# Attention and a gated expert on one core: the first span's later output products in hi and lo parts, two weight splits a block sooner, and a last output that ends row group by row group

## The chip, the core and the metric

The kernel runs on one core of a Trainium2 chip. A core has a matrix engine (TensorE, PE in the profile, with its weight loads as PEld), VectorE (DVE), ScalarE (ACT) and GpSimd (POOL), a queue engine for transfers (SyncE, SP), and 16 DMA engines between device memory and the on-chip memory. TensorE writes its sums into PSUM banks, from which the other engines read them. Each engine works through its own list of instructions in order and waits where an input isn't there yet. The metric is the device time of one execution in microseconds (us); lower is better.

## The reference

Linear attention over q, k and v, then a gated feed-forward layer over its output:

```python
def _attn_ref(q, k, v):                       # (8, 8, 576, 64) each
    q_s = np.exp(q - np.max(q, axis=-1, keepdims=True))
    q_s = q_s / (np.sum(q_s, axis=-1, keepdims=True) + 1e-09)
    k_s = np.exp(k - np.max(k, axis=2, keepdims=True))
    k_s = k_s / (np.sum(k_s, axis=2, keepdims=True) + 1e-09)
    kv = np.einsum('bhsd,bhse->bhde', k_s, v)
    return np.einsum('bhsd,bhde->bhse', q_s, kv).astype(np.float32)

def _moe_ref(x, w_gate, w_val, w_out):        # x: 4608 tokens x 512; d_ff 1536
    gate = 1.0 / (1.0 + np.exp(-(x @ w_gate)))
    val = x @ w_val
    return (gate * val @ w_out).astype(np.float32)
```

The attention's output of (8, 8, 576, 64) is laid out as 4608 tokens of 512 features. The weights arrive as float64 words.

## The kernel before

**Tiling.** The tokens are worked in 9 spans of 512 (`NW = 9`, `T = 512`), each of 4 row groups of 128 (`NT = 4`). The 1536 hidden features are 12 blocks of 128 (`NJ = 12`), or 6 pairs (`NS = 6`).

**First span and later spans differ.** The first span (w = 0) works while the weights arrive. It runs over the 12 blocks j = 0 to 11. `g1_0(j)` makes the gate and the value product of a block from plain float32 weights (line 650; 8 products, which the profile shows as 16 records), `g_sig_0(j)` (658, ScalarE) and `g_mul_0(j)` (662, VectorE) form the block's hidden values `h_0[j]`, and `g2_0(j)` (677) multiplies them with the block of the output weights, in float32, into four accumulators, one for each row group. The loop issues `g2_0(j - 1)` after `g1_0(j)`.

The later spans (w = 1 to 8) run over the pairs in `g1` (695) and `g2` (763). There every number is held as two parts that TensorE takes at its faster type float32r: hi, the number rounded by a cast on ScalarE, and lo, the remainder from a subtraction on VectorE. A product of two numbers is then three products, hi by hi, hi by lo and lo by hi. `g1` also uses a scheme of seven half-size products on sums of weight quarters (`w_sums`) instead of eight.

**What the first span does besides.** During the 12 blocks the weights are narrowed from float64 and got ready for the later spans, in this order around the change:

- `w_low`, `w_top`, `w_join` (lines 146, 153, 168, 175) narrow a block of the gate and value weights; `wo_low`, `wo_top`, `wo_join` a block of the output weights. Of these `w_top` and `wo_top` are on ScalarE, the others on VectorE.
- `wo_hi(j)` (224, ScalarE) and `wo_lo(j)` (228, VectorE) make the hi and lo parts of a block of output weights in a buffer `wo_hl` (two of them), `wo_store` writes them to device memory from POOL's queue; `wo_save` is `wo_lo` and `wo_store`.
- For each of the 6 pairs p, `w_sums(p)` (260, VectorE) makes four sums of weight quarters, and a split makes hi and lo parts of the four sums and of the three quarters used as they are: `split_hi(p)` (284, ScalarE) and `split_lo(p)` (289, VectorE), six casts and six subtractions. The parts of the sums go through one buffer, `s_sb`, and are stored from POOL's queue. The dictionary `splits` says in which block each split stands; `w_sums` of a split stands at the end of the block before.
- `beside_first(j)` and `after_first(j)` prepare span 1: `qT_split` (540, a cast on ScalarE; 541, a subtraction on VectorE), `x_mm` (565) and its eviction `x_ev` (573), transposes `qf_tr` (527), the k part of batch 2 (`k_max` 330, `k_sum` 337).
- The last two blocks, 10 and 11, are written out after the loop, with the sums and the split of the last pair (`w_sums(5)`, `split_hi(5, ...)`, `split_lo(5, ...)`; its six parts are `FIRST`, four `SUMS` and `LAST`) and the seven activations' parts `c_subs` (609), `c_split_hi` (625), `c_split_lo` (629) that span 1 begins with.

**What sets the order.** The order is written out by hand: each call appends its instructions to the engines' lists, and an engine never takes a later instruction first. Buffers come from pools with a fixed number of them; three PSUM banks (`ps_gv`) serve the gate and value products, the transposes and later `g1`'s three accumulators, and a new use waits until an earlier one has been read.

**The end.** `acc_out(w)` (669, 670) copies the four accumulators of a span on ScalarE and issues one transfer each from SP. In `g2` the loop over the two blocks of a pair is outside that over the four row groups, so that in the last pair the four accumulators are all finished by the last 12 products.

Of the kernel before, what the change touches and what calls it, by code (L numbers as in the profile page):

```python
# [52 lines left out]
def attn_moe(ctx: ExitStack, tc: tile.TileContext, qf, qn, qT, k, kT, v, wg, wv, wo, out):  # L53
# [156 lines left out]
    def wo_top(j):  # L210
        if j % 2 == 0:
            wo_t[j // 2] = wtpool.tile([P, 2, DM], F32, name="wo_t")
        if not wo_on_vector(j):
            narrow_sign(wo_raw[j])
        narrow_abs(wo_raw[j], wo_t[j // 2][:, j % 2])

    def wo_join(j):
        narrow_join(wo_raw.pop(j), wo_t[j // 2][:, j % 2])
# [3 lines left out]
    def wo_hi(j):  # L222
        wo_out[j] = t = whpool.tile([P, 2, DM], F32R, name="wo_hl")
        nc.scalar.copy(out=t[:, 0], in_=wo_t[j // 2][:, j % 2])

    def wo_lo(j):
        t = wo_out[j]
        nc.vector.tensor_tensor(
            out=t[:, 1], in0=wo_t[j // 2][:, j % 2], in1=t[:, 0].bitcast(F32), op=ALU.subtract
        )  # L230

    def wo_store(j):
        t = wo_out[j]
        nc.gpsimd.dma_start(out=wo_dram[j], in_=t.rearrange("p h e -> p (h e)").bitcast(F32))
# [43 lines left out]
    def split_hi(p, parts=(*SUMS, FIRST, LAST)):  # L278

        if p not in a_w:  # L280
            a_w[p] = apool.tile([P, 3, 2, 2, 2 * P], F32R, name="a_w", tag=f"a{p}")
        for part in parts:
            o, x = split_of(p)[part]
            nc.scalar.copy(out=o[:, :, 0], in_=x)

    def split_lo(p, parts=(*SUMS, FIRST, LAST)):
        for part in parts:
            o, x = split_of(p)[part]
            nc.vector.tensor_tensor(
                out=o[:, :, 1], in0=x, in1=o[:, :, 0].bitcast(F32), op=ALU.subtract  # L290
            )
            if part in SUMS:
                i = part - 1
                nc.gpsimd.dma_start(
                    out=s_dram[p][:, i * 8 * P:(i + 1) * 8 * P],
                    in_=s_sb[:, i].rearrange("p h n e -> p (h n e)").bitcast(F32),
                )
# [307 lines left out]
    def c_subs():  # L605

        def sub(i, x, y):
            c_32[i] = t = ring.tile([P, 2, HT], F32, name="ring")
            nc.vector.tensor_tensor(out=t, in0=x, in1=y, op=ALU.subtract)

        sub(T1, quarter(0, 1), quarter(0, 0))
        sub(T2, quarter(1, 1), c_32[T1])
        sub(T3, quarter(1, 1), quarter(0, 1))
        sub(T4, quarter(1, 0), c_32[T2])
# [29 lines left out]
    def g1_0(j):  # L644
# [8 lines left out]
                )  # L653
        gate[j] = ps

    def g_sig_0(j):
        h_0[j] = two.tile([P, T], F32, name="h_0", tag="h_lo")
        nc.scalar.activation(h_0[j], gate[j][0], AF.Sigmoid)

    def g_mul_0(j):  # L660
        g = h_0[j]
        nc.vector.tensor_tensor(out=g, in0=gate.pop(j)[1], in1=g, op=ALU.mult)

    def acc_new(w):
        acc[w] = [ps_acc.tile([P, DM], F32, name="acc") for _ in range(NT)]

    def acc_out(w):
        for m in range(NT):
            nc.scalar.copy(out=x_32[:, m], in_=acc[w][m])
            nc.sync.dma_start(out=out[w * T + m * P:w * T + (m + 1) * P], in_=x_32[:, m])  # L670
        del acc[w]

    def g2_0(j):
        if j == 0:
            acc_new(0)
        for m in range(NT):
            nc.tensor.matmul(  # L677
                acc[0][m], lhsT=h_0[j][:, m * P:(m + 1) * P], rhs=wo_t[j // 2][:, j % 2],
                start=(j == 0), stop=(j == NJ - 1),
            )  # L680
        if j == NJ - 1:
            acc_out(0)

# [70 lines left out]
    def g2(w, at):  # L754
        p = step(w, at)
        if at == 0:
            acc_new(w)
        h, o = h_hl.pop((w, p)), wo_hl.pop((w, p))
        for i in range(2):
            for m in range(NT):  # L760
                sl = slice(m * P, (m + 1) * P)
                for lh, rh in ((0, 0), (0, 1), (1, 0)):
                    nc.tensor.matmul(  # L763
                        acc[w][m], lhsT=h[lh][:, i, sl], rhs=o[i][:, rh],
                        start=(at == 0 and i == 0 and lh == 0 and rh == 0),
                        stop=(at == NS - 1 and i == 1 and lh == 1),
                    )
        if at == NS - 1:
            acc_out(w)

# [257 lines left out]
    for t in range(5):  # L1028
        k_load(1, t)

    splits = {2: 0, 5: 1, 7: 2, 9: 3, 10: 4, 11: 5}
    for j in range(NJ - 2):
        g1_0(j)
        beside_first(j)
        split = splits.get(j)
        if split is not None:
            split_hi(split)
        if j == 0:
            g_sig_0(j)
        else:  # L1040
            wo_hi(j - 1)
            g_mul_0(j - 1)
        w_top(j + 2)
        if j > 0:
            g_sig_0(j)
        w_join(j + 1)
        wo_top(j + 1)
        wo_join(j)
        if j + 3 < NJ:
            w_low(j + 3)  # L1050
        wo_low(j + 2)
        if j > 0:
            wo_save(j - 1)
        if j + 3 < NJ:
            load_wo(j + 3)
        if j + 5 < NJ - 1:
            load_w(j + 5)
        if j == 7:
            load_w(NJ - 1)
        if split is not None:  # L1060
            split_lo(split)
        if j + 1 in splits:
            w_sums(splits[j + 1])
# [8 lines left out]
    beside_first(j)  # L1072
    wo_hi(j - 1)
    g_mul_0(j - 1)
    wo_top(j + 1)
    split_hi(4)
    wo_lo(j - 1)
    wo_store(j - 1)
    w_join(j + 1)
    wo_join(j)  # L1080
    g_sig_0(j)
    split_lo(4)
    k_max_read(2)
    c_split_hi(B11)
    wo_hi(j)
    g_mul_0(j)
    wo_join(j + 1)
    g2_0(j - 1)

    g1_0(j + 1)  # L1090
    w_sums(5)
    split_hi(5, (FIRST,))
    g_sig_0(j + 1)
    split_hi(5, SUMS)
    c_subs()
    load_next(1, 5, range(2))
    c_split_lo(B11)
    split_lo(5, (FIRST,))
    split_lo(5, SUMS[0:1])
    c_split(T1)  # L1100
    g_mul_0(j + 1)
    split_lo(5, SUMS[1:2])
    c_split(T2)
    c_split(B21)
    wo_save(j)
    split_lo(5, SUMS[2:3])
    c_split(T3)
    split_lo(5, SUMS[3:4])
# [1 line left out]
    split_hi(5, (LAST,))  # L1110
    split_lo(5, (LAST,))
    c_split(T4)
    wo_hi(j + 1)
    wo_lo(j + 1)
    g2_0(j)
    for t in range(2, 5):
        v_load(2, t)

    def wo_next(w, at):
# [71 lines left out]
```

## Time and profile before

| | |
|---|---|
| median of 3 runs | 944.86 us (944.68 to 947.01) |
| profiled execution, its own time | 946.96 us |
| its span, first to last instruction | 945.2 us |
| mean granted TensorE clock | 0.994 |
| TensorE busy (PE) | 933.5 us, 99% of the span |
| VectorE busy | 626.4 us, 66% |
| ScalarE busy | 485.4 us, 51% |
| GpSimd busy | 176.5 us, 19% |
| first span's last output product of the loop, block 9, starts | at 148.91 us |
| span 1's products start | at 162.64 us |

The busy shares are means over the whole span. In the first span, some 160 us, VectorE and ScalarE are much busier than in the rest. The chain of waits that the page gives is followed back from the last instruction; a line of it says how much of the span lies on an engine's work. Line numbers of rows are those of the kernel before.

### The profile page before, as it was taken

Reading aid. Unit: us, or ns where it says so; the run is one execution under the profiler, and the core shown is the slowest. Engines: PE = TensorE matmul, PEld = TensorE weight load, DVE = VectorE, ACT = ScalarE, POOL = GpSimd, SP = SyncE. Lnnn points to the kernel's source line nnn. Section 1 sums busy time; section 2 is a strip of 40 time slices with the busy share of each in tenths; the row PEclk is TensorE's granted clock in tenths of the full one; section 3 lists DMA queues with packets and bytes.
Section 4 is the critical chain, followed back from the end, with each engine's and each line's share of the span. In section 5 each row is a group of like instructions: output and inputs, shape, how many; then the busy total and the mean of one; then the engine's idle time right before and its main releaser. Section 6 shows DMA issues by size and latency. Waiting matters only on the chain.

```text
span 945.2 us, 15707 instructions
## 1 busy us (share of the span) xinstructions
PE 933.5 (99%) x6062; PEld 808.2 (86%) x6062; DVE 626.4 (66%) x1017; ACT 485.4 (51%) x822; POOL 176.5 (19%) x330
## 2 busy tenths in 40 slices
PE   6999999999999999999999999999999999999998
PEld 5545545899999999999999999999999999999997
DVE  8899879874767477755776568556856664654242
ACT  4799786635455445544563456254725443543222
POOL 0011112222121212212221122112212122222220
PEclk8999999999999999999999999999999999999999
DMA  9996576999699969996999699978997789858661
GB/s 323 328 392 226 210 288 237 362 342 272 185 372 320 264 183 354 335 266 208 333 331 283 204 309 344 287 246 252 351 266 229 221 258 314 238 177 262 212 212 67
DMA packets 94249, 256.74 MB, mean 272 GB/s; under 512 B 13600, under 2 KB 15904, under 8 KB 94176
## 3 DMA queue, kind: packets, MB, share of 16 engines
q0 software_dynamic: 46016, 167.27, 56.6%
q1 hardware_dynamic: 48160, 88.48, 30.9%
q8 instruction: 48, 0.79, 0.4%
q14 instruction: 25, 0.20, 0.1%
HBM read 227.15 MB, written 28.56 MB: 271 GB/s over the span
## 4 chain that ended last, share of the span: by engine, by line
PE 98%; DVE 1%; DMA 1%; ACT 0%; issue 0%; SPq 0%; DVEq 0%
PE gv L695 49%; PE acc L763 28%; PE gv L650 9%; PE acc L677 4%; PE at L405 3%; PE gv L565 2%; PE at L565 1%; PE acc L392 1%; DMA lent<-k_in 1%; PE acc L589 0%; PE gv L527 0%; DVE lent L480 0%; DVE q_m L473 0%; DVE lent L963 0%; ACT lent L384 0%; ACT lent L484 0%
## 5 line engine op out<-in xcount | busy, mean ns | idle before, releaser
L695 PE MATMUL gv<-c_hl,s_sb 128*128 128x256 f32 x2304 | 277.6, 276 | 0.0
L695 PEld LDWEIGHTS gv<-c_hl,s_sb 128*128 128x128 f32 x2304 | 269.1, 188 | 0.0
L695 PE MATMUL gv<-c_hl,a_w 128*128 128x256 f32 x1728 | 221.0, 277 | 0.0
L695 PEld LDWEIGHTS gv<-c_hl,a_w 128*128 128x128 f32 x1728 | 210.5, 188 | 4.6 <-issue 0.7
L301 POOL DMA_DIRECT2D s_sb<-s x188 | 101.3, 539 | 306.2 <-PE gv L695 299.8
L721 DVE TENSOR_TENSOR sg<-gv,sg 128x512 f32<-128x512 f32 x48 | 33.2, 691 | 167.5 <-PE gv L695 167.5
L763 PE MATMUL acc<-wo_hl,h 128*128 128x512 f32 x588 | 142.4, 391 | 0.0
L763 PE MATMUL acc<-wo_t,h 128*128 128x512 f32 x564 | 138.9, 394 | 0.0
L763 PEld LDWEIGHTS acc<-wo_t,h 128*128 128x128 f32 x564 | 105.8, 188 | 24.8
L763 PEld LDWEIGHTS acc<-wo_hl,h 128*128 128x128 f32 x588 | 106.9, 188 | 20.7
L713 ACT COPY sg<-gv 128x512 f32<-128x512 f32 x48 | 28.1, 585 | 118.1 <-PE gv L695 104.7
L723 ACT COPY sg<-gv 128x512 f32<-128x512 f32 x48 | 28.2, 587 | 102.8 <-PE gv L695 102.8
L725 DVE TENSOR_TENSOR sg<-sg 128x512 f32<-128x512 f32 x48 | 33.2, 692 | 57.1 <-ACT sg L723 57.1
L650 PE MATMUL gv<-x,f_w 128*128 128x512 f32 x160 | 70.3, 593 | 0.0
L248 POOL DMA_DIRECT2D wo_hl<-wo x47 | 27.6, 588 | 194.8 <-PE acc L763 194.8
L650 PEld LDWEIGHTS gv<-x,f_w 128*128 128x128 f32 x160 | 30.0, 190 | 36.6 <-issue 34.4
L746 DVE TENSOR_TENSOR h<-sg,h 128x1024 fp32r<-128x1024 f32 x48 | 58.8, 1226 | 1.6
L734 DVE TENSOR_TENSOR sg<-sg 128x512 f32<-128x512 f32 x48 | 33.2, 692 | 33.5 <-ACT sg L728 33.5
L728 ACT ACTIVATE sg<-sg 128x512 f32<-128x512 f32 x48 | 30.3, 632 | 46.1 <-DVE sg L727 46.1
L718 ACT COPY sg<-gv 128x512 f32<-128x512 f32 x48 | 28.2, 587 | 37.3 <-PE gv L695 37.3
L715 ACT COPY sg<-gv 128x512 f32<-128x512 f32 x48 | 28.2, 587 | 36.5 <-PE gv L695 36.5
L248 POOL DMA_DIRECT2D wo_t<-wo x47 | 25.3, 538 | 99.2 <-PE acc L763 99.1
(153 smaller groups left out, 1151.3 us busy)
## 6 DMA issues: line engine op xcount, KB each, us to landing
s_sb<-s POOLq DMA_DIRECT2D x188, 512.0 KB, 6.2
wo_hl<-wo POOLq DMA_DIRECT2D x47, 512.0 KB, 5.0
wo_t<-wo POOLq DMA_DIRECT2D x47, 512.0 KB, 6.6
s<-s_sb POOLq DMA_DIRECT2D x24, 512.0 KB, 6.7
out<-x SPq DMA_DIRECT2D x36, 256.0 KB, 7.0
ring<-k_in SPq DMA_DIRECT2D x28, 256.0 KB, 9.5
ring<-qn_in SPq DMA_DIRECT2D x28, 256.0 KB, 6.0
q_b<-q_m_row SPq DMA_DIRECT2D x56, 128.0 KB, 9.4
```

The lines of the kernel that those rows point to most:

```text
L248: nc.gpsimd.dma_start(out=t.rearrange("p h e -> p (h e)"), in_=wo_dram[2 * p + i].bitcast(F32R))
L301: nc.gpsimd.dma_start(out=s_sb[:, i].rearrange("p h n e -> p (h n e)"), in_=s_dram[p][:, i * n:(i + 1) * n].bitcast(F32R),)
L405: nc.tensor.matmul(kvps[b][:, hp], lhsT=kt[:n, sl], rhs=vt[:n, sl], start=(t == 0 and hp == 0), stop=(t == len(KTILES) - 1 and hp == NP - ...
L650: nc.tensor.matmul(ps[n], lhsT=w[:, kt // 2, sl], rhs=x_0[:, kt], start=(kt == 0), stop=(kt == NK - 1),)
L677: nc.tensor.matmul(acc[0][m], lhsT=h_0[j][:, m * P:(m + 1) * P], rhs=wo_t[j // 2][:, j % 2], start=(j == 0), stop=(j == NJ - 1),)
L695: nc.tensor.matmul(ps[:, n], lhsT=lh(kt), rhs=c_hl[i][:, x, kt], start=(first and n == 0 and kt == 0 and lh is wh and x == 0), stop=(last ...
L721: nc.vector.tensor_tensor(out=sg[:, 0], in0=rr, in1=sg[:, 0], op=ALU.add)
L725: nc.vector.tensor_tensor(out=sg[:, 3], in0=sg[:, 3], in1=sg[:, 2], op=ALU.add)
L728: nc.scalar.activation(sg[:, 0:2, 0], sg[:, 0:2, 0], AF.Sigmoid)
L734: tt(out=sg[:, 0:2, 0], in0=sg[:, 0:2, 0], in1=sg[:, 0:2, 1], op=ALU.mult)
L746: nc.vector.tensor_tensor(out=lo, in0=sg[:, :, 0], in1=hi.bitcast(F32), op=ALU.subtract)
L763: nc.tensor.matmul(acc[w][m], lhsT=h[lh][:, i, sl], rhs=o[i][:, rh], start=(at == 0 and i == 0 and lh == 0 and rh == 0), stop=(at == NS - ...
```

## The change

It has three parts.

1. For the blocks j = 6 to 11 of the first span (`IN_PARTS = 6`), `g2_0(j)` uses hi and lo parts like the later spans: 12 products of float32r where there were 4 of float32. The hidden values get hi and lo parts for it: `h_hi_0(j)`, a cast on ScalarE, and `h_lo_0(j)`, a subtraction on VectorE. The output weights' parts are those that `wo_hi` and `wo_lo` make anyway. `wo_save(j - 1)` stands earlier in the block for these. `h_0[j]` lies in one of two tiles that held v rows; their two loads for batch 2 move behind the first span's last steps.
2. The splits of the pairs 3 and 4 move from the blocks 9 and 10 to the blocks 8 and 9, and with them their sums; in these two blocks `split_hi` stands later, behind `wo_join` and `h_lo_0`. The order of the blocks 10 and 11 is written anew around them.
3. In the last `g2` of the last span the loop over the row groups is outside, and each row group is copied and sent as soon as it is finished (`acc_out_of`); the last one is copied in two halves, one on ScalarE and one on VectorE, with a transfer each.

```diff
+    IN_PARTS = 6
+
     def g_sig_0(j):
-        h_0[j] = two.tile([P, T], F32, name="h_0", tag="h_lo")
+        h_0[j] = v_two[j % 2] if j >= IN_PARTS else two.tile([P, T], F32, name="h_0", tag="h_lo")
         nc.scalar.activation(h_0[j], gate[j][0], AF.Sigmoid)
...
+    def h_hi_0(j):
+        if j >= IN_PARTS:
+            h_parts[j] = t = two.tile([P, 2, T], F32R, name="h_parts", tag="h_lo")
+            nc.scalar.copy(out=t[:, 0], in_=h_0[j])
+
+    def h_lo_0(j):
+        if j >= IN_PARTS:
+            hi, lo = (h_parts[j][:, i] for i in range(2))
+            nc.vector.tensor_tensor(out=lo, in0=h_0[j], in1=hi.bitcast(F32), op=ALU.subtract)
...
+    def acc_out_of(w, m):
+        rows = out[w * T + m * P:w * T + (m + 1) * P]
+        if w == NW - 1 and m == NT - 1:
+            for i, copy in enumerate((nc.scalar.copy, nc.vector.tensor_copy)):
+                half = slice(i * HT, (i + 1) * HT)
+                copy(out=x_32[:, m, half], in_=acc[w][m][:, half])
+                nc.sync.dma_start(out=rows[:, half], in_=x_32[:, m, half])
+        else:
             nc.scalar.copy(out=x_32[:, m], in_=acc[w][m])
-            nc.sync.dma_start(out=out[w * T + m * P:w * T + (m + 1) * P], in_=x_32[:, m])
-        del acc[w]
+            nc.sync.dma_start(out=rows, in_=x_32[:, m])
 
     def g2_0(j):
         if j == 0:
             acc_new(0)
+        if j < IN_PARTS:
+            pairs = [(h_0[j], wo_t[j // 2][:, j % 2])]
+        else:
+            hi, lo = (h_parts[j][:, i] for i in range(2))
+            o = wo_out[j]
+            pairs = [(hi, o[:, 0]), (hi, o[:, 1]), (lo, o[:, 0])]
         for m in range(NT):
-            nc.tensor.matmul(
-                acc[0][m], lhsT=h_0[j][:, m * P:(m + 1) * P], rhs=wo_t[j // 2][:, j % 2],
-                start=(j == 0), stop=(j == NJ - 1),
-            )
+            for i, (h, o) in enumerate(pairs):
+                nc.tensor.matmul(
+                    acc[0][m], lhsT=h[:, m * P:(m + 1) * P], rhs=o,
+                    start=(j == 0), stop=(j == NJ - 1 and i == len(pairs) - 1),
+                )
...
+        if w == NW - 1 and at == NS - 1:
+            for m in range(NT):
+                part(0, m)
+                part(1, m)
+                acc_out_of(w, m)
+            return
...
-    splits = {2: 0, 5: 1, 7: 2, 9: 3, 10: 4, 11: 5}
+    splits = {2: 0, 5: 1, 7: 2, 8: 3, 9: 4}
     for j in range(NJ - 2):
         g1_0(j)
         beside_first(j)
         split = splits.get(j)
-        if split is not None:
+        if split is not None and j < 8:
             split_hi(split)
         if j == 0:
             g_sig_0(j)
         else:
             wo_hi(j - 1)
             g_mul_0(j - 1)
+            h_hi_0(j - 1)
         w_top(j + 2)
         if j > 0:
             g_sig_0(j)
         w_join(j + 1)
         wo_top(j + 1)
         wo_join(j)
+        if j > 0:
+            h_lo_0(j - 1)
+        if split is not None and j >= 8:
+            split_hi(split)
+        if j > IN_PARTS:
+            wo_save(j - 1)
         if j + 3 < NJ:
             w_low(j + 3)
         wo_low(j + 2)
-        if j > 0:
+        if 0 < j <= IN_PARTS:
             wo_save(j - 1)
...
@@ block 10
     wo_hi(j - 1)
     g_mul_0(j - 1)
+    h_hi_0(j - 1)
     wo_top(j + 1)
-    split_hi(4)
-    wo_lo(j - 1)
-    wo_store(j - 1)
+    wo_save(j - 1)
     w_join(j + 1)
     wo_join(j)
+    h_lo_0(j - 1)
+    k_max_read(2)
     g_sig_0(j)
-    split_lo(4)
-    k_max_read(2)
     c_split_hi(B11)
     wo_hi(j)
-    g_mul_0(j)
-    wo_join(j + 1)
-    g2_0(j - 1)
-
-    g1_0(j + 1)
     w_sums(5)
     split_hi(5, (FIRST,))
+    g_mul_0(j)
+    h_hi_0(j)
+    split_hi(5, SUMS[0:2])
+    c_subs()
+    load_next(1, 5, ())
+    wo_join(j + 1)
+    wo_save(j)
+    h_lo_0(j)
+    c_split_lo(B11)
+    g2_0(j - 1)
+
+    g1_0(j + 1)
+    split_hi(5, SUMS[2:4])
+    c_split_hi(T1)
     g_sig_0(j + 1)
-    split_hi(5, SUMS)
-    c_subs()
-    load_next(1, 5, range(2))
-    c_split_lo(B11)
     split_lo(5, (FIRST,))
     split_lo(5, SUMS[0:1])
-    c_split(T1)
+    c_split_lo(T1)
     g_mul_0(j + 1)
+    h_hi_0(j + 1)
+    wo_hi(j + 1)
     split_lo(5, SUMS[1:2])
     c_split(T2)
     c_split(B21)
-    wo_save(j)
...
     c_split(T4)
-    wo_hi(j + 1)
+    h_lo_0(j + 1)
     wo_lo(j + 1)
     g2_0(j)
-    for t in range(2, 5):
+    for t in range(5):
         v_load(2, t)
```

More of the change, by code (lines that the diff above doesn't have):

```diff
@@ L662, in g_mul_0 @@
         nc.vector.tensor_tensor(out=g, in0=gate.pop(j)[1], in1=g, op=ALU.mult)
+    h_parts = {}
+    def h_hi_0(j):
[6 more added lines that the diff above has]
+            nc.vector.tensor_tensor(out=lo, in0=h_0[j], in1=hi.bitcast(F32), op=ALU.subtract)
     def acc_new(w):
@@ L668, in acc_out @@
         for m in range(NT):
+            acc_out_of(w, m)
+        del acc[w]
+    def acc_out_of(w, m):
[6 more added lines that the diff above has]
+        else:
             nc.scalar.copy(out=x_32[:, m], in_=acc[w][m])
-            nc.sync.dma_start(out=out[w * T + m * P:w * T + (m + 1) * P], in_=x_32[:, m])
-        del acc[w]
+            nc.sync.dma_start(out=rows, in_=x_32[:, m])
     def g2_0(j):
@@ L758, in g2, with part @@
         h, o = h_hl.pop((w, p)), wo_hl.pop((w, p))
+        def part(i, m):
+            sl = slice(m * P, (m + 1) * P)
+            for lh, rh in ((0, 0), (0, 1), (1, 0)):
+                nc.tensor.matmul(
+                    acc[w][m], lhsT=h[lh][:, i, sl], rhs=o[i][:, rh],
+                    start=(at == 0 and i == 0 and lh == 0 and rh == 0),
+                    stop=(at == NS - 1 and i == 1 and lh == 1),
+                )
+        if w == NW - 1 and at == NS - 1:
+            for m in range(NT):
+                part(0, m)
+                part(1, m)
+                acc_out_of(w, m)
+            return
         for i in range(2):
             for m in range(NT):
[L761 to L767, printed above, removed]
+                part(i, m)
         if at == NS - 1:
@@ L1074, in attn_moe @@
     g_mul_0(j - 1)
+    h_hi_0(j - 1)
     wo_top(j + 1)
-    split_hi(4)
-    wo_lo(j - 1)
-    wo_store(j - 1)
+    wo_save(j - 1)
     w_join(j + 1)
     wo_join(j)
+    h_lo_0(j - 1)
+    k_max_read(2)
     g_sig_0(j)
-    split_lo(4)
-    k_max_read(2)
     c_split_hi(B11)
     wo_hi(j)
+    w_sums(5)
+    split_hi(5, (FIRST,))
     g_mul_0(j)
+    h_hi_0(j)
+    split_hi(5, SUMS[0:2])
+    c_subs()
+    load_next(1, 5, ())
     wo_join(j + 1)
+    wo_save(j)
+    h_lo_0(j)
+    c_split_lo(B11)
     g2_0(j - 1)
     g1_0(j + 1)
-    w_sums(5)
-    split_hi(5, (FIRST,))
+    split_hi(5, SUMS[2:4])
+    c_split_hi(T1)
     g_sig_0(j + 1)
-    split_hi(5, SUMS)
-    c_subs()
-    load_next(1, 5, range(2))
-    c_split_lo(B11)
     split_lo(5, (FIRST,))
     split_lo(5, SUMS[0:1])
-    c_split(T1)
+    c_split_lo(T1)
     g_mul_0(j + 1)
+    h_hi_0(j + 1)
+    wo_hi(j + 1)
     split_lo(5, SUMS[1:2])
```

## The prediction

> **What bounds the kernel now.** I read the page's span and its chain of waits first, then the chain in order of time.
>
> ```profile
> span 945.2 us, 15707 instructions
> ...
> PE 98%; DVE 1%; DMA 1%; ACT 0%; issue 0%; SPq 0%; DVEq 0%
> ```
>
> The chain runs on TensorE for 98% of the span. So a TensorE microsecond saved is a microsecond won, as long as the work that feeds TensorE stays ahead of it. In order of time (start, duration, what):
>
> ```profile
> 118.92 7.06 PE gv L650 x16
> 125.97 3.43 PE acc L677 x8
> ...
> 130.79 6.87 PE gv L650 x16
> ...
> 148.91 3.43 PE acc L677 x8
> ...
> 200.87 4.66 PE at L405 x40
> ...
> 211.26 9.52 PE gv L695 x84
> 220.78 5.53 PE acc L763 x24
> ...
> 941.52 0.59 ACT x L669
> ```
>
> L650 is the gate and value product of a block of the first span, L677 its output product. The one at 125.97 belongs to block 7 (they lag by one block), the one at 148.91 to block 9. TensorE has no gap here, but its feeders have little slack. Two stretches of the windows view (columns: window, length, then busy time of PE, PEld, DVE, ACT, POOL):
>
> ```profile
> 106.87:120.44 13.57, 13.57 (x42) 6.83 (x41) 9.47 (x15) 13.55 (x20) 2.65 (x5) 1.00 0.59 213
> ...
> 131.49:168.24 36.75, 36.75 (x128) 19.96 (x127) 36.54 (x60) 26.06 (x42) 10.03 (x19) 1.00 0.69 241
> ```
>
> ScalarE (ACT) is busy for 13.55 of 13.57 us through block 7, VectorE (DVE) for 36.54 of 36.75 from block 9 to the second span. These are the stretches into which the change puts work.
>
> **The change, part by part.** *Output products.* A block's 4 products of L677 take 3.43 us (8 records); 24 products with hi and lo parts take 5.53 (L763), so the new 12 take 2.77. That is 0.66 less per block, 4.0 for six.
>
> The Trainium skill ("TensorE: Matmul & The Clock Gate", section "Back-to-back issue gap") gives some 131 ns for a sustained 512-column product. By it the 12 would take 1.6 and the gain would be an estimated 11 us; the row's 230 ns per product decides against it.
>
> *What feeds them.* Each of the six blocks gets one more cast on ScalarE (h_hi_0) and one more subtraction on VectorE (h_lo_0). The new part is the order. ScalarE's cast waits for VectorE's product g_mul_0, and everything else of that block on ScalarE stands behind it; from block 8 on the split's casts come at the end of ScalarE's list, and VectorE's subtractions wait for those. Each engine keeps its order, so I follow the two lists in turn. ScalarE's rows:
>
> ```profile
> 111.38 0.62 ACT L224 CAST wo_hl<-wo_t 128x512 fp32r<-128x512 f32 x1
> ...
> 120.44 0.56 ACT L573 COPY x<-at 128x512 f32<-128x512 f32 x1
> 120.91 0.58 ACT L540 CAST ring<-gv 128x512 fp32r<-128x512 f32 x1
> 121.39 0.62 ACT L224 CAST wo_hl<-wo_t 128x512 fp32r<-128x512 f32 x1
> 121.91 2.51 ACT L153 ACTIVATE sg<-sg 128x1024 f16<-128x1024 f32 x1
> ...
> 127.27 0.67 ACT L168 ACTIVATE wo_t<-wo_raw 128x512 f32<-128x512 f32 x1
> ...
> 135.41 2.51 ACT L153 ACTIVATE w_raw<-w_raw 128x1024 f16<-128x1024 f32 x1
> ...
> 140.38 0.71 ACT L168 ACTIVATE wo_t<-wo_raw 128x512 f32<-128x512 f32 x1
> ```
>
> VectorE's:
>
> ```profile
> 110.99 0.69 DVE L146 TENSOR_SCALAR sg<-sg 128x1024 uint32<-128x1024 uint32 x1
> ...
> 115.67 1.82 DVE L289 TENSOR_TENSOR a_w<-f_w,a_w 128x1024 fp32r<-128x1024 f32 x2
> 121.53 0.69 DVE L541 TENSOR_TENSOR ring<-gv,ring 128x512 fp32r<-128x512 f32 x1 [4.04 <-ACT ring L540]
> 122.13 0.68 DVE L662 TENSOR_TENSOR h<-gv,h 128x512 f32<-128x512 f32 x1
> ...
> 136.20 2.48 DVE L289 TENSOR_TENSOR s_sb<-s,s_sb 128x512 fp32r<-128x512 f32 x4
> ...
> 140.34 0.68 DVE L260 TENSOR_TENSOR s<-f_w 128x512 f32<-128x512 f32 x1
> ...
> 142.88 0.74 DVE L330 TENSOR_REDUCE k_max<-kt 128x1 f32<-128x576 f32 x1
> ...
> 144.58 0.69 DVE L662 TENSOR_TENSOR h<-gv,h 128x512 f32<-128x512 f32 x1
> ...
> 147.59 2.49 DVE L289 TENSOR_TENSOR s_sb<-s,s_sb 128x512 fp32r<-128x512 f32 x4
> ...
> 152.94 0.68 DVE L260 TENSOR_TENSOR s<-f_last 128x512 f32<-128x512 f32 x1
> ...
> 155.47 0.68 DVE L609 TENSOR_TENSOR ring<-x 128x512 f32<-128x512 f32 x1
> ...
> 158.00 0.68 DVE L629 TENSOR_TENSOR c_hl<-x,c_hl 128x512 fp32r<-128x512 f32 x1
> ```
>
> From starts: a ScalarE cast takes 0.52 (121.39 to 121.91), a VectorE subtraction 0.60 (121.53 to 122.13). A split's six subtractions take 4.14 (136.20 to 140.34), a set of sums 2.54 (140.34 to 142.88).
>
> Block 7. ScalarE has no room, so the added cast puts the copy at 120.44 to 120.96 and the query's cast behind it to 121.43, ending 122.0. VectorE: it is free for h_lo_0 at 110.99, but the new cast ends only at 111.38+0.52+0.62 = 112.5, a wait of 1.5; with h_lo_0 (0.6) the split ends at 117.5+2.1 = 119.6, and the third split's sums, moved here, end at 122.2. The idle 4.04 us of this row was the cover; it is used up.
>
> Block 8. The query's subtraction at 122.2, block 7's product 122.8 to 123.4, ScalarE's cast of it then (0.52), and ScalarE's work from 121.91 to 127.27+0.58 = 127.85 (5.94) behind it: the third split's casts begin at 129.9, the first ends at 130.5. After its product VectorE has joins (1.8), h_lo_0 and wo_lo (1.2) and narrowing (0.9), is free at 127.3 and idles 3.2. Then 4.14 of subtractions and 2.54 of sums: 137.2. Only then comes the subtraction that block 9 begins with, which TensorE needs: a PSUM bank has to come free for the second half of a block's gate and value products. This row shows that it is the bank which L541 reads (it ends at 122.22):
>
> ```profile
> 122.27 0.30 PEld L650 LDWEIGHTS gv<-x,f_w 128*128 128x128 f32 x2 [0.75 <-DVE ring L541]
> ```
>
> In block 8 TensorE comes there 0.66 sooner than before, and L541 ends at 122.9 instead of 122.22: a stall longer by 1.1 to 1.3. In block 9 it reached that half at 130.79+3.43 = 134.2; two shorter output products and the longer stall leave about 134. It must wait until L541 ends at 137.9: **a stall of 3.9**.
>
> Block 9. Product 137.8 to 138.5, cast 0.52, then ScalarE's 135.41 to 140.38+0.58 (5.55): the fourth split's casts begin at 144.6, the first ends at 145.2. VectorE, free at 142.3, idles 2.9; then 4.14, the two maxima 1.70 (142.88 to 144.58): 151.1. In block 10 product, wo_lo and three joins take 3.01 (144.58 to 147.59), h_lo_0 0.69: 154.8. **The output product of block 9 starts at 154.85 instead of 148.91**, 5.94 later; TensorE has been idle for 2.9 before it. The stalls of blocks 8 and 9 and this one lie inside the number, as do three shorter output products.
>
> From there TensorE runs on: the three other shorter output products give back 2.0, so +3.95. One more wait: VectorE from 154.7 does the last sums 2.53 (152.94 to 155.47), a product 0.6, the differences 2.53 (155.47 to 158.00), four operations 2.4, then about 2.3 (large first part, two small ones): 165.1; block 11's product ends at 165.8. ScalarE's cast h_hi_0(11) waits for it with seven casts behind, and only then comes the eviction of the second span's first product: 165.8+8*0.52 = 170.0, done 170.6. TensorE asks for it at 154.85+2.77+6.87+2.77+2*1.36 = 170.0 (84 products in 9.52 make 1.36 for twelve). **+0.65**; its ends are 0 and 1.3.
>
> *Moves on other queues.* The splits share one s_sb buffer that POOL stores; a store lands after
>
> ```profile
> s<-s_sb POOLq DMA_DIRECT2D x24, 512.0 KB, 6.7
> ```
>
> so the stores of the second split (last small subtraction done at about 118) land by 126, 4 us before the third split's casts; the third's by about 141, ahead of 144.6. If that cover went, its lateness would add to VectorE's wait one for one. POOL's wo_store moves ahead, with no one waiting. On SP two v loads move behind the k loads and wait for h_lo_0(11), about 173; their reader, the second batch's k products, is at 200.87 before: hidden.
>
> *Last rows.* Products in another order end at the same time. The last copy, 0.59 at 941.52, becomes two halves side by side and two transfers:
>
> ```profile
> 172.42 0.36 ACT L732 ACTIVATE sg<-gv 128x256 f32<-128x256 f32 x1
> ...
> L670 SPq DMA_DIRECT2D out<-x x4: 332/333/333, 940.0 to 942.1; - x4
> ```
>
> A half takes about 0.4 by that row (0.2 less), the second issue comes 0.33 after the first (so 0.13 later than now), and half the bytes land sooner: between +0.2 and -0.6, I take -0.2.
>
> **Sum:** 3.95 + 0.65 - 0.2 = +4.4. The profiled execution took 946.96 (span 945.2 and 1.8 around it) and would take 951.4; it lay 2.1 above the median, so the median goes from 944.86 to **949.3**.
>
> **The rivals.** *The clock drops (0.15).* Granted clock, third column from the right, at the start of the kernel:
>
> ```profile
> 12.00:14.00 2.00, 0.37 (x1) 0.00 (x0) 2.00 (x4) 0.99 (x2) 0.00 (x0) 1.00 1.22 291
> 14.00:16.00 2.00, 0.00 (x0) 0.00 (x0) 1.38 (x3) 0.83 (x3) 0.00 (x0) 0.89 1.27 279
> 16.00:18.00 2.00, 1.20 (x4) 0.93 (x4) 1.97 (x4) 2.00 (x5) 0.00 (x0) 0.50 0.95 360
> ...
> 24.00:26.00 2.00, 2.00 (x11) 1.79 (x10) 1.60 (x4) 0.00 (x0) 0.00 (x0) 0.55 1.06 393
> ```
>
> TensorE has no work from 12.4 on; after 3.2 us the clock halves (about 15.6) and comes back at about 25.8. My stall of 3.9 is long enough for that. Up to 10.2 us at half rate cost up to 5.1, of which 2.9 lie under the wait for block 9's output product: 1 to 2.2 more, 950.3 to 951.5. It needs the idle time to fall right, hence the low chance. The Trainium skill (same page, section "Part 1: The HAM clock gate (the "warmup" mystery)") has a free-running window of 3.4 us behind this, so that not every stall of 3.9 would trip it; the rows above agree on the length.
>
> *Fewer hold-ups (0.14).* If the fourth split's casts don't hold VectorE up for 2.9, block 9's output product is ready when TensorE comes. Then 1.1 and 3.9 of stalls stand against 4.0 and 0.2 saved, and the last wait of 0.65 is gone: +0.8, 945.7. If the third split's casts didn't hold it up for its 3.2 either, block 9's stall would be 0.7: -2.4, 942.5, still inside 0.3%. Against it: ScalarE's work before those casts is 5.55 long and begins only after the late product.
>
> *Faster (0.05).* The other side: ScalarE's casts are always there before VectorE asks. Then all three waits of VectorE, 1.5 + 3.2 + 2.9 = 7.6, are gone, L541 comes in time in blocks 8 and 9, and the saving stands whole: 944.86-4.0-0.2 = 940.7. It decides once about 7 of the 7.6 are gone. The idle 4.04 before L541, which shows room on VectorE, speaks for it; ScalarE's 13.55 busy of 13.57 us speaks against it.
>
> **How the numbers follow.** My case 0.66 (own range 948.2 to 950.5, from 0 to 1.3 at the last wait, the ends of the last rows, and 0.5 for hand-overs). 0.3% is 2.8 us, about what a measurement of this kernel can tell from no change: slower 0.81, same 0.14, faster 0.05. The range reaches down to the first of the cases without change, 945.5, and up past the clock case, 951.8.
>
> **What would show it.** In the changed profile: output products of blocks 6 to 11 at 2.77 each; VectorE idle some 3 us ahead of the subtractions of the third and the fourth split, released by ScalarE's casts; TensorE idle nearly 4 us in the middle of block 9's gate and value products and nearly 3 ahead of block 9's output product; the second span starting 4 to 5 us later. I am wrong if the split's casts on ScalarE begin near 126 in block 8, if TensorE has no gap between 130 and 160, or if the granted clock dips there.

## The result: slower, by 5.3 us in its own schedule and by 7.45 us in the medians

| | before | after |
|---|---|---|
| six runs, us | 944.68, 944.78, 944.86, 945.12, 946.64, 947.01 | 950.12, 950.20, 952.23, 952.65, 952.98, 953.01 |
| median | 944.99 | 952.44 |
| profiled execution, span | 946.96, 945.2 | 950.20, 948.4 |
| mean granted clock of the profiled execution | 0.994 | 0.996 |

The ratio is 1.0067 [1.0051, 1.0084], which is also that of the mean times, 951.87 to 945.52; the medians differ by 7.45 us, 0.79%. The forecast was 949.3 with a range of 945.5 to 951.8, from a median before of 944.86: the right side, 3 us too low. The measured median lies 0.6 above the range's end; the ratio, put on 944.86, gives 951.2, inside it. Two executions in the experiments, of 965.57 us (kernel before) and 1905.48 us (e4), are left out of what is compared.

The runs of a kernel lie in groups two to three microseconds apart, and the mean granted clock goes with them: 0.996 in the lower group of both kernels, 0.994 (before) and 0.993 (after) in the upper. At the start, while TensorE has no work, the clock halves; before's profile has it halved from 15.6 to 25.8 us. The windows view of after (columns as in the prediction, the clock third from the right) has a shorter stretch, from 14.2 to 21.0:

```profile
14.00:15.00 1.00, 0.00 (x0) 0.00 (x0) 1.00 (x2) 0.00 (x0) 0.00 (x0) 0.59 1.19 292
...
20.00:21.00 1.00, 1.00 (x5) 0.77 (x5) 1.00 (x2) 1.00 (x1) 0.00 (x0) 0.50 1.00 397
21.00:22.00 1.00, 1.00 (x8) 0.88 (x8) 0.90 (x4) 1.00 (x2) 0.00 (x0) 0.99 1.01 401
```

Everything behind it stands 2.44 us early in after's trace. The change isn't the reason: e5 below, whose first span is that of the kernel before, has the short stretch too and stands 2.50 early. The 3.4 us less at half rate account for at most 1.7 of this; the rest stays open. The first of the added work comes behind block 6's first gate product, so I measure from there to span 1's first output product: *the stretch*. Before (TensorE in order of time: start, duration, what):

```profile
95.38 3.17 PE L650 MATMUL gv<-x,f_w 128*128 128x512 f32 x7
...
167.94 2.88 PE L695 MATMUL gv<-c_hl,s_sb 128*128 128x256 f32 x24
...
185.37 5.60 PE L763 MATMUL acc<-wo_hl,h 128*128 128x512 f32 x24
```

After, with the waits in brackets (idle time before, and what ended it):

```profile
92.94 3.60 PE L650 MATMUL gv<-x,f_w 128*128 128x512 f32 x8
...
120.42 3.70 PE L650 MATMUL gv<-x,f_w 128*128 128x512 f32 x8 [1.18 <-DVE ring L541]
...
135.55 3.70 PE L650 MATMUL gv<-x,f_w 128*128 128x512 f32 x8 [3.89 <-DVE ring L541]
...
150.23 0.73 PE L708 MATMUL acc<-wo_hl,h_parts 128*128 128x512 f32 x2 [0.42 <-ACT h_parts L671]
152.59 2.56 PE L708 MATMUL acc<-wo_hl,h_parts 128*128 128x512 f32 x10 [1.62 <-DVE h_parts L676]
...
168.38 1.68 PE L726 MATMUL gv<-c_hl,s_sb 128*128 128x256 f32 x12 [0.76 <-ACT sg L744]
...
171.31 2.99 PE L726 MATMUL gv<-c_hl,s_sb 128*128 128x256 f32 x24
...
175.55 2.93 PE L708 MATMUL acc<-wo_hl,h_parts 128*128 128x512 f32 x12
...
181.69 1.65 PE L726 MATMUL gv<-c_hl,s_sb 128*128 128x256 f32 x12 [0.38 <-ACT sg L744]
...
188.61 5.62 PE L794 MATMUL acc<-wo_hl,h 128*128 128x512 f32 x24
```

The stretch was 185.37 - 95.38 = 89.99 and is 188.61 - 92.94 = 95.67: **+5.68**. TensorE's six gaps in it sum to 8.25, with some 0.2 more each time until the pipelined products run at pace again; six shorter output products give back 4.0. To the third pair's k products (*the long stretch*, 107.11 before) it is +5.69, so nothing comes behind it, and the spans, each from its own start, give 948.4 + 2.44 - 945.2 = +5.64. The runs agree: after's two at mean clock 0.996 lie 5.3 above before's four in their lower group. The other 2.1 of the medians' 7.45 is the grouping: four of six runs of after, two of before, lie in the upper group. With six runs that is partly chance: in the experiments' three batches 13 of 28, 10 of 23 and 5 of 13 runs of the kernel before lie above 946 us.

The page's chain of waits moved with it. TensorE carried 98% of it, and VectorE 1%; in after:

```profile
PE 90%; DVE 5%; ACT 3%; issue 1%; DMA 1%; SPq 0%; ACTq 0%; DVEq 0%
```

### The profile page after: what moved, and what is told of

Its sections match the earlier page's. It is cut to its first block, busy times and chain, and to the rows that moved or that the text cites. A ratio compares the mean times of both kernels' runs of the same rounds, so it can differ in the third digit from the quotient of the medians.

```text
span 948.4 us, 15770 instructions
## 1 busy us (share of the span) xinstructions
PE 929.8 (98%) x6086; PEld 811.5 (86%) x6086; DVE 630.6 (66%) x1024; ACT 488.3 (51%) x828; POOL 177.2 (19%) x330
## 4 chain that ended last, share of the span: by engine, by line
PE 90%; DVE 5%; ACT 3%; issue 1%; DMA 1%; SPq 0%; ACTq 0%; DVEq 0%
PE gv L726 48%; PE acc L794 28%; PE gv L650 5%; PE at L405 3%; PE acc L708 2%; PE gv L565 2%; DVE s L260 1%; DVE a_w L289 1%; PE acc L392 1%; DVE s_sb L289 1%; PE at L565 1%; DMA lent<-k_in 1%; PE acc L589 0%; DVE v L664 0%; ACT c_hl L625 0%
## 5 line engine op out<-in xcount | busy, mean ns | idle before, releaser
L794 PE MATMUL acc<-wo_hl,h 128*128 128x512 f32 x588 | 143.0, 391 | 0.0
```

Source lines behind the costliest of these rows:

```text
L794: nc.tensor.matmul(acc[w][m], lhsT=h[lh][:, i, sl], rhs=o[i][:, rh], start=(at == 0 and i == 0 and lh == 0 and rh == 0), stop=(at == NS - ...
```

## The experiments

A theory and a rival stood at the outset. Theory A is the prediction's: the loss is hand-overs between two in-order lists, with the place of the casts on ScalarE as its cause. Rival B: the loss is the added work, wherever it stands, since VectorE was nearly full already. The first expectations name a rival C as well: the blocks 8 and 9 are too early for these two splits, wherever in them the casts stand. Edits are against the changed kernel where nothing else is said. Runs of one batch shared the runs of the kernel before; stretches are compared with 89.99 and 107.11.

**Without the parts (e2).** Only the two moved splits, the new order of the blocks 10 and 11 and the last rows are left.

```diff
-    IN_PARTS = 6
+    IN_PARTS = NJ
```

> The changed kernel without hi and lo parts in the first span (all its output products in float32 as before); the splits' new places, the new order and the last rows stay. Theory A: the late casts alone cost part of the loss. VectorE still waits in block 8 (some 2.3 us), TensorE has a gap of 1.8 in block 9, no wait for a cast of hidden values is left: +1.8 in the stretch against before. Rival B (the added work): 0 or a gain, since no work is added. Rival C (the splits' new blocks): the full +5.7 or more, as the products are longer too.

946.94 us, ratio 1.0016 [1.0005, 1.0028], stretch +2.06. TensorE and VectorE of this run:

```profile
136.08 3.70 PE L650 MATMUL gv<-x,f_w 128*128 128x512 f32 x8 [1.76 <-DVE ring L541]
...
128.56 2.50 DVE L289 TENSOR_TENSOR s_sb<-s,s_sb 128x512 fp32r<-128x512 f32 x4 [2.31 <-ACT s_sb L284]
```

The sums and splits alone, a block sooner, with the new order around them, lose 2 us: VectorE waits 2.31 for the third split's casts, and TensorE 1.76 for VectorE. Here theory A was right to 0.3; B's 0 or a gain and C's 5.7 were not met.

**Three blocks with parts instead of six (e4).**

```diff
-    IN_PARTS = 6
+    IN_PARTS = 9
```

> The changed kernel with hi and lo parts only for the blocks 9 to 11 (three instead of six). Theory A: no hidden-value cast stands in ScalarE's list in the crowded blocks 7 and 8, so the chain of hand-overs has only the split's late casts left: +0.4 against before. Rival B (added work): half of the work, so about half of the loss, +2.8. Rival C: +5.7 with three longer products, some +7.

Its eleven comparable runs have a median of 946.14 us; ratio 1.0007 [0.9995, 1.0019], stretch +1.07. B asked for 2.8. Parts in blocks 9 to 11 even give back 1.0 of what the splits cost alone (2.0 would be the whole saving of three shorter output products), so added work in these three blocks isn't the loss. A was 0.7 too low.

**The new cast on VectorE (e3).** It adds work to VectorE and takes away the hand-over; it also takes six casts of 0.52 us off ScalarE.

```diff
-            nc.scalar.copy(out=t[:, 0], in_=h_0[j])
+            nc.vector.tensor_copy(out=t[:, 0], in_=h_0[j])
```

> The changed kernel with the cast of the hidden values (h_hi_0) on VectorE instead of ScalarE: the work on VectorE grows by six casts (about 0.35 us each by the 0.69 of a cast twice as wide), ScalarE's list no longer waits for VectorE's product. Theory A: the stretch falls from +5.7 to about +0.6, since ScalarE runs ahead again and its split casts come 2 to 4 us sooner. Rival B (VectorE simply has too much to do): it rises by the six casts, to about +7.8. Rival C: unchanged, +5.7.

948.28 us, ratio 1.0021 [1.0009, 1.0034], stretch +1.27. B's +7.8 is refuted: with six more operations on VectorE, 4.4 of the 5.68 are gone, and C's unchanged 5.7 wasn't met either. Since ScalarE also has less to do here, the run doesn't tell the hand-over from ScalarE's load; e10 below leaves the load as it is. What is left is mostly a wait at another place:

```profile
137.13 3.27 PE L650 MATMUL gv<-x,f_w 128*128 128x512 f32 x7 [2.91 <-ACT v L660]
...
135.53 0.68 DVE L541 TENSOR_TENSOR ring<-gv,ring 128x512 fp32r<-128x512 f32 x1
...
136.50 0.58 ACT L660 ACTIVATE v<-gv 128x512 f32<-128x512 f32 x1
```

Block 9's second half goes on when ScalarE's sigmoid has read the product of its first half (136.50 + 0.58 = 137.08), not when L541 is done (136.21). Which reader holds a block up changed with the order of the others.

**The splits' casts at the head of the block (e1).** If the casts stand too late, put them first, as the earlier splits have them.

```diff
-        if split is not None and j < 8:
+        if split is not None:
             split_hi(split)
...
-        if split is not None and j >= 8:
-            split_hi(split)
```

> The changed kernel, with the third and the fourth split's casts put at the head of ScalarE's list in blocks 8 and 9 instead of behind the output weights' join. I compare the stretch from block 6's first gate product to span 1's first output product: 90.0 us before the change, 95.7 with it (5.7 more). Theory A (the lists hand over too late: VectorE waits 3.1 and 2.7 us for those casts): nearly all of it goes. Following both lists with the trace's durations I get +0.9 over the kernel before, so about 4.5 to 5 us less than the changed kernel, with VectorE's two waits gone and TensorE's gap of 3.9 in block 9 below 1. Rival B (the added casts and subtractions themselves are too much, whatever their order): the stretch stays at +5.7. Rival C (block 8 and 9 are too early for these splits): it stays too, or gets longer.

950.82 us, ratio 1.0054 [1.0035, 1.0072], stretch +6.76: a plain miss for A, which asked for +0.9. By its number alone it is what B and C asked for (+5.7, or for C longer). ScalarE in order of time shows another reason:

```profile
122.05 0.62 ACT L284 CAST s_sb<-s 128x512 fp32r<-128x512 f32 x1 [0.87 <-DMA s<-s_sb]
...
133.47 0.62 ACT L284 CAST s_sb<-s 128x512 fp32r<-128x512 f32 x1 [0.59 <-DMA s<-s_sb]
...
135.54 0.62 ACT L284 CAST s_sb<-s 128x512 fp32r<-128x512 f32 x1 [1.45 <-DMA s<-s_sb]
...
137.72 0.62 ACT L284 CAST s_sb<-s 128x512 fp32r<-128x512 f32 x1 [1.57 <-DMA s<-s_sb]
```

The casts write `s_sb`, of which there is one, and wait there for the stores of the split before. Behind them in ScalarE's list stands the cast of block 8's hidden values, and TensorE waits for that:

```profile
140.90 0.50 PE L708 MATMUL acc<-wo_hl,h_parts 128*128 128x512 f32 x1 [2.43 <-ACT h_parts L671]
...
142.22 4.36 PE L708 MATMUL acc<-wo_hl,h_parts 128*128 128x512 f32 x11 [0.82 <-DVE wo_hl L228]
```

The late place of the casts wasn't only a loss: it covered a third party, the store. The prediction had priced this ("its lateness would add to VectorE's wait one for one"), but my theory left it out. (The 4.36 for eleven products, 2.77 at full rate, is a clock drop from 143.0 to 146.4 in this profile, which lengthens them by 1.6. The miss doesn't rest on it: the three fastest runs of e1, 950.04 to 950.41, are no faster than after's 950.12 and 950.20.)

**The third split first, the fourth in between (e10).** Six blocks with parts. The fourth split's casts stand behind `w_top` in block 9, which gives the store time and still comes before the rest of ScalarE's block.

```diff
-        if split is not None and j < 8:
+        if split is not None and j < 9:
             split_hi(split)
...
         w_top(j + 2)
+        if j == 9:
+            split_hi(4)
...
-        if split is not None and j >= 8:
-            split_hi(split)
```

> The changed kernel with all six blocks, the third split's casts at the head of block 8, and the fourth's in block 9 behind w_top instead of at the head. Theory: in the version with both at the head the fourth split's casts waited three times (0.6, 1.5 and 1.6 us) for the third split's stores out of the one s_sb buffer, with the hidden values' cast behind them. Here the stores have landed, ScalarE's three waits go, and the stretch falls from +6.8 to about +2.5; what is left is block 8, where the casts at the head hold up block 7's hidden values. Rival B (work, not order): it stays near +5.7.

948.15 us, ratio 1.0031 [1.0020, 1.0042], stretch +3.32 (0.8 above the expectation): 2.4 of the 5.68 lay in the place of these casts. ScalarE does the same work as in the changed kernel, so this much is order, not load, and B's +5.7 is refuted. In block 9 the casts no longer wait for a transfer; in block 8 they still do, and behind it TensorE waits 1.42 for block 7's hidden values:

```profile
122.59 0.62 ACT L284 CAST s_sb<-s 128x512 fp32r<-128x512 f32 x1 [1.17 <-DMA s<-s_sb]
...
125.77 0.49 PE L708 MATMUL acc<-wo_hl,h_parts 128*128 128x512 f32 x1 [1.42 <-ACT h_parts L671]
```

**The last casts behind (e6).** `h_hi_0(11)` and `wo_hi(11)` come after the casts of the last activation, so that ScalarE's list no longer stands still for block 11's product.

```diff
-    h_hi_0(j + 1)
-    wo_hi(j + 1)
...
     c_split(T4)
+    h_hi_0(j + 1)
+    wo_hi(j + 1)
```

> The changed kernel with block 11's two casts (hidden values' h_hi_0(11), output weights' wo_hi(11)) moved behind the casts that span 1's first pair needs. Theory: ScalarE's wait of 4.2 us for VectorE's product no longer stands before these six casts; the wait of 0.8 us for the eviction of the second span's first product goes, the rest of the loss stays: stretch +5.1 instead of +5.7. Rival: that wait is made up for by the next one anyway (the eviction in the second pair), and the stretch stays at +5.7.

950.72 us, ratio 1.0051 [1.0035, 1.0067], stretch +4.95: the wait for span 1's first eviction is gone, 0.73 of the stretch; 0.6 was expected. This profile shows what a clock drop in block 9's gap does. TensorE, then the windows view:

```profile
138.17 5.40 PE L650 MATMUL gv<-x,f_w 128*128 128x512 f32 x8 [3.88 <-DVE ring L541]
...
155.21 2.58 PE L708 MATMUL acc<-wo_hl,h_parts 128*128 128x512 f32 x10 [0.62 <-DVE h_parts L676]
```

```profile
140.00:141.00 1.00, 1.00 (x3) 0.48 (x2) 1.00 (x2) 1.00 (x1) 0.00 (x0) 0.50 0.00 0
```

Half rate from 139.2 to 142.6 stretches the eight records from 3.70 to 5.40. But the wait for block 9's output product shrinks from 0.42 + 1.62 to 0.62, and the stretch is no longer for it. Most of a drop in this gap lies under the next wait.

**Two sums of k later (e7).** The k exponentials of steps 2 and 3 (batch 2) move out of ScalarE's list ahead of the second pair's first eviction, one step on.

```diff
                 k_sub(b, 0); k_sub(b, 1)
-                k_sum(b, 2); k_sum(b, 3)
+                if n > 2:
+                    k_sum(b, 2); k_sum(b, 3)
         if p == 1:
+            if n == 2:
+                k_sum(b, 2); k_sum(b, 3)
```

> The changed kernel with the two exponentials of k for batch 2 (and their table load) moved from between span 1's first and second pair to the next step. Theory: they stand in ScalarE's list before the second pair's first eviction, for which TensorE waits there since the last output product of the first span is shorter: that wait of some 0.5 us goes and the stretch is +5.2 instead of +5.7. Rival: the four copies of the first span's sums set that wait by themselves; then nothing changes.

950.87 us, ratio 1.0054 [1.0040, 1.0068]. The stretch is +5.01, but the long stretch +5.78. TensorE:

```profile
169.23 1.65 PE L726 MATMUL gv<-c_hl,s_sb 128*128 128x256 f32 x12 [0.75 <-ACT sg L744]
...
197.71 1.68 PE L726 MATMUL gv<-c_hl,s_sb 128*128 128x256 f32 x12 [0.50 <-ACT sg L744]
```

The second pair's 0.38 is gone and 0.50 stands in the third pair: a wait moved by one pair, not removed.

**The last rows alone (e5).** The kernel before with part 3 only: `acc_out_of` and the loop over row groups outside in the last `g2`.

```diff
+        if w == NW - 1 and at == NS - 1:
+            for m in range(NT):
+                part(0, m)
+                part(1, m)
+                acc_out_of(w, m)
+            return
```

> The kernel before with the third part alone: the last output run ends row group by row group, the last one in two halves. The first span is untouched (stretch 90.0). Expected from the changed kernel's trace: VectorE's half begins only when ScalarE's has ended, so the end after TensorE's last product stays at about 3.6 us against 3.7: no change that can be measured, 0 to 0.2 us less. If this part mattered for the loss, it would be 1 us or more longer here.

944.46 us, ratio 0.9993 [0.9983, 1.0004], stretch 89.98: no measurable difference, so parts 1 and 2 carry the whole loss.

**The gap filled (e11).** Fourteen products that nothing uses, 128 by 128, stand in block 9's gap, to see whether the clock drop there makes the upper group of runs.

```diff
+            if j == 9 and n == 0:
+                d = ps_at.tile([P, P], F32, name="at")
+                for _ in range(14):
+                    nc.tensor.matmul(d, lhsT=ident, rhs=ident, start=True, stop=True)
```

> The changed kernel with 14 needless 128x128 products (of the identity with itself, some 3.0 us, into a free PSUM bank) in TensorE's gap in the middle of block 9. They fill 3.0 of its 3.9 us and put nothing behind them. Theory (the clock): with TensorE at work there, the granted clock isn't halved after the gap; its profile shows 1.00 from 30 us on, and the runs near 952 to 953 of the changed kernel that had a mean granted clock of 0.993 don't come back: median near 950.5. Rival: those runs come from the start of the kernel alone, where the clock is at half rate for 6.8 or 10.2 us; then the median stays near 952.

951.64 us, ratio 1.0067 [1.0052, 1.0081]. No better: 950.5 was missed. TensorE was kept busy through the gap, but the clock halved after the next one, from 153.9 to 157.4 (TensorE's rows, then the windows view):

```profile
131.92 3.39 PE L657 MATMUL at<-ident 128*128 128x128 f32 x28
135.91 3.70 PE L650 MATMUL gv<-x,f_w 128*128 128x512 f32 x8 [0.60 <-DVE ring L541]
...
152.96 3.81 PE L712 MATMUL acc<-wo_hl,h_parts 128*128 128x512 f32 x10 [1.62 <-DVE h_parts L680]
```

```profile
155.00:156.00 1.00, 1.00 (x4) 0.81 (x3) 1.00 (x3) 0.00 (x0) 0.00 (x0) 0.50 0.68 152
```

This drop costs: 3.81 against 2.56 for the ten products, and the stretch is +6.62, 0.94 more than in the changed kernel, though the wait of 0.76 for span 1's first eviction is gone.

**The pieces together, twice (e8, e9).** First (e8): parts in blocks 8 to 11, the second split in block 6 instead of 7, the third and fourth at the head of 8 and 9, last casts behind, k sums later.

```diff
-    IN_PARTS = 6
+    IN_PARTS = 8
...
-    splits = {2: 0, 5: 1, 7: 2, 8: 3, 9: 4}
+    splits = {2: 0, 5: 1, 6: 2, 8: 3, 9: 4}
```

> A version to beat both: hi and lo parts for the blocks 8 to 11, the second split (with its sums) at the end of block 6 where ScalarE and VectorE idle 4.2 and 3.3 us, the third and fourth split's casts at the head of blocks 8 and 9, block 11's casts behind those that span 1 needs, the two exponentials of batch 2 a step later, and the last rows as in the change. Theory A: all waits of TensorE in the first span are gone, so four shorter products (0.66 each) show in full: stretch -2.6 against before, time about 2.7 us less (0.3%). Rival B (added work sets the loss): four of six blocks still cost, +2 to +4.

945.67 us, ratio 1.0001 [0.9990, 1.0013], stretch -0.25 against an expected -2.6 (long stretch +0.25). ScalarE shows the store again, in the block where two splits follow each other directly:

```profile
133.02 0.62 ACT L284 CAST s_sb<-s 128x512 fp32r<-128x512 f32 x1 [0.37 <-DMA s<-s_sb]
...
135.53 0.62 ACT L284 CAST s_sb<-s 128x512 fp32r<-128x512 f32 x1 [1.90 <-DMA s<-s_sb]
```

Then (e9): as e8, but the fourth split's casts behind `w_top` as in e10, the k sums where they were, and two of span 0's four copies on VectorE.

```diff
-            nc.scalar.copy(out=x_32[:, m], in_=acc[w][m])
+            copy = nc.vector.tensor_copy if w == 0 and m % 2 else nc.scalar.copy
+            copy(out=x_32[:, m], in_=acc[w][m])
...
         w_top(j + 2)
+        if j == 9:
+            split_hi(4)
```

> A second version to beat both: hi and lo parts for the blocks 8 to 11; second split with its sums at the end of block 6; third split's casts at the head of block 8; the fourth split's casts in block 9 behind the narrowing of block 11 (w_top), so that the stores of the third split's parts have landed by then and the hidden values' cast isn't behind them; block 11's casts behind those that span 1 needs; of the four copies of the first span's sums two on VectorE, so that ScalarE reaches the second pair's first eviction sooner; last rows as in the change. Theory A with the store as third party: no wait of TensorE is left in the stretch and four shorter products show, -2.6 in the stretch, some 942.3 in all. Rival B (the added work sets it): no better than the earlier version of four blocks, whose stretch to span 1's second pair was 0.25 shorter than before and whose time was no different.

**942.64 us** (942.32 to 944.70), ratio **0.9967 [0.9955, 0.9979]** to the kernel before: below both kernels, by 2.3 and 9.8 us of the medians (944.94 for the kernel before in this batch; the changed kernel's 952.44 is from the first). The stretch is 182.65 - 95.23 = 87.42, that is -2.57, as expected. TensorE has one wait left between block 6 and the third pair, and VectorE's wait for the fourth split is small:

```profile
182.65 5.60 PE L795 MATMUL acc<-wo_hl,h 128*128 128x512 f32 x24
...
191.60 1.65 PE L727 MATMUL gv<-c_hl,s_sb 128*128 128x256 f32 x12 [0.53 <-ACT sg L745]
...
137.11 2.50 DVE L289 TENSOR_TENSOR s_sb<-s,s_sb 128x512 fp32r<-128x512 f32 x4 [0.58 <-ACT s_sb L284]
```

That wait takes back 0.53 (long stretch -2.02). So the shorter products are real, and can be had where the hand-overs and the store leave room. The third and fourth split stand in the blocks 8 and 9 here too, which refutes C as the reason by itself. What isn't shown is the same for six blocks: no run with six blocks and the casts on ScalarE got below +3.32, and how much of that is order and how much the engines' load stays open. e9 also differs from e8 in three things at once, so the trace, not the time, tells what each did.

## Why the prediction was right in its steps and 3 us too low

Both lists came out as followed by hand. VectorE, then ScalarE of the changed kernel:

```profile
110.12 0.69 DVE L676 TENSOR_TENSOR h_parts<-v,h_parts 128x512 fp32r<-128x512 f32 x1 [1.47 <-ACT h_parts L671]
...
128.03 2.50 DVE L289 TENSOR_TENSOR s_sb<-s,s_sb 128x512 fp32r<-128x512 f32 x4 [3.11 <-ACT s_sb L284]
...
134.81 0.68 DVE L541 TENSOR_TENSOR ring<-gv,ring 128x512 fp32r<-128x512 f32 x1
...
142.90 2.50 DVE L289 TENSOR_TENSOR s_sb<-s,s_sb 128x512 fp32r<-128x512 f32 x4 [2.72 <-ACT s_sb L284]
...
151.85 0.68 DVE L676 TENSOR_TENSOR h_parts<-v,h_parts 128x512 fp32r<-128x512 f32 x1
```

```profile
127.39 2.16 ACT L284 CAST s_sb<-s 128x512 fp32r<-128x512 f32 x4
...
142.24 2.18 ACT L284 CAST s_sb<-s 128x512 fp32r<-128x512 f32 x4
...
163.58 0.62 ACT L671 CAST h_parts<-v 128x512 fp32r<-128x512 f32 x1 [4.17 <-DVE v L664]
...
167.76 0.57 ACT L744 COPY sg<-gv 128x512 f32<-128x512 f32 x1
...
179.12 2.02 ACT L694 COPY x<-acc 128x512 f32<-128x512 f32 x4
181.02 0.61 ACT L744 COPY sg<-gv 128x512 f32<-128x512 f32 x1
```

| step of the prediction | forecast | measured (times + 2.44) |
|---|---|---|
| block 7: VectorE waits for the new cast | 1.5 | 1.47 |
| block 8: the third split's casts begin | 129.9 | 127.39 + 2.44 = 129.83 |
| block 8: VectorE idles for them | 3.2 | 3.11 |
| block 8: TensorE's stall | 1.1 to 1.3 | 1.18 |
| block 9: L541 ends | 137.9 | 134.81 + 0.68 + 2.44 = 137.93 |
| block 9: TensorE's stall | 3.9 | 3.89 |
| block 9: the fourth split's casts; VectorE idles | 144.6; 2.9 | 144.68; 2.72 |
| `h_lo_0(9)` ends | 154.8 | 151.85 + 0.68 + 2.44 = 154.97 |
| span 1's first eviction: wait | 0.65 | 0.76 |

Ahead of block 9's output product TensorE idles 0.42 + 1.62 instead of 2.9, since the two hi by hi products of its first row group slip in; the lo products, which set the time, came as forecast.

The sum was 4.6 for the stretch and it measures 5.68. Four terms make up 1.0 of the difference:

- `h_lo_0(9)` 0.17 later, and the eviction's wait 0.11 longer.
- Span 1's first pair runs at a slower pace, 2.99 for a record group of 24 (171.31) against 2.88 before (167.94): 7.17 us from the wait's end to the output product instead of 6.81 for the same products, **+0.36**. The prediction priced twelve products at 1.36; five groups of twelve took 1.41 (0.25 of it), the first of them 1.52 right after the wait (0.11).
- "The three other shorter output products give back 2.0" was too much: block 11's gives 13.35 - 13.06 = 0.29 of its 0.66 up to span 1's output product, because TensorE now comes 0.38 too early for the second pair's first eviction (the copies at 179.12 stand ahead of the one at 181.02). **+0.37**: a saving that ran into the next wait. (The wait and the restart behind it cost some 0.6; the products after it run at 1.36 where before's ran at 1.41, which gives 0.2 back.) In e7, where this wait is gone, the same stretch is 188.78 - 176.15 = 12.63, and the whole saving stands.

The rest, 0.07, stays unassigned. The last rows were forecast at -0.2. The two halves of the last copy, on ScalarE, then on VectorE:

```profile
944.81 0.37 ACT L691 COPY x<-acc 128x256 f32<-128x256 f32 x1 [0.81 <-PE acc L794]
...
945.21 0.42 DVE L691 COPY x<-acc 128x256 f32<-128x256 f32 x1 [8.11 <-ACT x L691]
```

The halves ran one behind the other, not side by side. From the first copy's start to the end it is 948.4 - 944.81 = 3.59, where it was 945.2 - 941.52 = 3.68: -0.1. Whether the shared bank or the shared destination tile orders them wasn't tried.

So the schedule's price was 5.3 to 5.6 instead of 4.4, and the rest of the medians' difference is the grouping of the runs, which the prediction didn't speak of. It took over how before's profile and median lie to each other; that four of six runs of after came to lie in the upper group was bad luck for it, in part at least. Among the profiles, those with 6.8 us at half rate there have block 6's first gate product at 92.9 to 93.8, those with 10.2 at 95.2 to 95.7. After's upper group lies 2.1 to 2.9 above its lower at a mean clock of 0.993, which makes about 13.6 us at half rate: 10.2 at the start and one 3.4 in a gap, as e6's profile has them, would fit both numbers (e7's profile has 6.8 and 6.8 and the same mean clock, but its second stretch lies mostly under the wait and couldn't lift a run by 2). No profile of such a run of after was taken, so this is inferred.

The rival of the dropping clock had the wrong price and chance. Its drops do occur (e1, e6, e7 and e11 show them, after's own profile doesn't), so 0.15 looks too low. But the "1 to 2.2 more" of a drop in block 9's gap was worked out for 10.2 us at half rate, and the drops in gaps are 3.4 or 6.8 us long: e6's drop of 3.4 us costs 1.7, and 1.4 of it goes under the wait for block 9's output product, which leaves 0.3.

The rival of fewer hold-ups is refuted for this kernel, and e10 shows its sign to be right: casts that come sooner win 2.4. The faster one isn't reached with six blocks; its mechanism is, in e9, with four. What neither rival had is that casts moved ahead meet the store of `s_sb`.

## What to carry to other kernels

Where two engines work through lists written by hand and each waits for the other, follow both lists instruction by instruction with the trace's issue intervals; here that gave the waits to a few tenths of a microsecond before the result was seen, and it failed in e1, where the store was left out of it. Before moving a late producer ahead, ask what its lateness covers: a single buffer with a store behind it can turn the move into a wait in the middle of that engine's list (e1, e8), while a place a few instructions later loses nothing to the store (block 9 in e9 and e10). And sum a saving only up to the next wait: 0.4 here, 0.5 in e7 and e9 came back one pair later.

## What the runs showed of the hardware

**The clock's drops.** In the profiles the stretches at half rate are 3.4, 6.8 or 10.2 us long. The Trainium skill ("TensorE: Matmul & The Clock Gate", section "Part 1: The HAM clock gate (the "warmup" mystery)") has a free-running window of about 3.4 us, and the lengths agree with it. It also has half rate come after at least one idle window, and there the rows differ: in e11 the clock fell at 153.9 with TensorE idle for about 1.65 of the 3.4 us before, in e1 after gaps of 2.43 and 0.82, while after's gap of 3.89 was followed by full rate:

```profile
136.00:137.00 1.00, 1.00 (x4) 0.44 (x3) 1.00 (x3) 0.87 (x2) 0.00 (x0) 1.00 0.58 234
```

What decides stays open.

**Two paces of one kind of product.** Twelve products of 128x256 take 1.36 or 1.41 us at full granted clock, and a pace is kept over many groups. Span 1's first pair begins at 1.41 in all ten profiles whose block 11 has parts, and at 1.36 in the three where its output product is in float32 (before, e2, e5). In four (e1, e4, e7, e11) it turns to 1.36 within that pair. What sets the pace stays open.
